# Three small edits to an attention and MLP block: a PSUM buffer, the place of twelve matmuls, and a quarter of an add on GpSimd

## The chip, the cores and the metric

The kernel runs on one core of a Trainium2 chip. The metric is the device time of one execution in microseconds (us), the median over several executions. A single core has no dies to compare, so a run here counts as fast unless it lies over 1.5% above the fastest of its kernel, which none did; the state of e7, which ran once, is unknown.

## The reference, cut to what matters

```
mod = (silu(c) @ w_mod).reshape(...)          # sa, ca, ga, sb, cb, gb, each 512 long
h = layernorm(x) * (1 + ca) + sa              # x is 2048 x 512
q = h @ wq                                    # 32 heads of 128
o = softmax(q k^T / sqrt(128)) v              # 8 groups of keys and values, 2048 keys
x = x + ga * (o @ wo)
h = layernorm(x) * (1 + cb) + sb
z = gelu(h @ w_in)                            # 1792 wide: halves z1, z2
g = w_sp @ layernorm(z2) + b_sp
x = x + gb * ((z1 * g) @ w_out)
```

## The kernel before

Attention is cut into 128 units, one for each group of keys (8) and tile of 128 query rows (16). A unit has 8 slots. In a slot PE (TensorE) writes two score blocks for this unit, ACT (ScalarE) takes their exponential, PE multiplies earlier exponentials of the unit before with the values, and then come "fill" matmuls that belong to something else:

```python
for it in range(NU + 6):
    ...
    for i in range(NSLOT):                       # NSLOT = 8
        for fn in later.pop((it, i), []):
            fn()
        if it < NU:
            qk(it, i)                            # 2 score matmuls, then exp on ACT
        if 1 <= it <= NU:
            pv(it - 1, i)                        # 8 value matmuls
        for fn in fill.pop((it, i), []):
            fn()                                 # projections, warm-up and the like
```

PSUM has three tags, each with two buffers: `misc` and `o_ps` (one bank each) and `s_ps` (two banks). Who takes a buffer waits until the reader of that buffer's last content is done.

```python
psum = fast.enter_context(tc.tile_pool(name="psum", bufs=2, space=bass.MemoryType.PSUM))
def bank(name):
    return psum.tile([P, 512], FP32, name=name)
```

Three places matter. First, in unit 0 normalised rows are turned (transposed) on PE, in two halves, and DVE (VectorE) scales each half on its way to SBUF:

```python
def ln1_turn(j0, n, xns):
    ...
    for half in range(2):
        t_ps = bank("misc")[:].bitcast(BF16).rearrange("p (k q) -> p k q", k=2)
        for k in range(2):
            ...
            nc.tensor.transpose(...)             # line 827
        for k in range(2):
            ln1_mod(dst, src, dt)                # line 809, DVE
```

Second, the queries of units 2 and 3 are projected by sixteen matmuls, `rest_q`, on line 940. The eighth and the sixteenth are each followed by a DVE cast into `qT` (line 951). Four run in unit 0, the others are fill of unit 1:

```python
rest_q = qproj(0, [0, 1], 2 * P, 2 * P) + qproj(0, [2, 3], 2 * P, 2 * P)
fill[0, 7] = rest_q[0:4]
for i in range(6):
    fill[1, i] = rest_q[4 + 2 * i : 6 + 2 * i]
```

Third, the end of each output tile:

```python
nc.vector.tensor_tensor(out=tmp[:], in0=src, in1=gb_rows[:], op=ALU.mult)       # src in PSUM
nc.vector.tensor_tensor(out=yout[:], in0=tmp[:], in1=x_sb[:, j, :], op=ALU.add)
nc.scalar.dma_start(out=out_dram[:, j, :], in_=yout[:])
```

## Time and profile before

| | before |
|---|---|
| median of 3 runs | 1321.84 us (1321.56 to 1321.89) |
| span of the profiled run | 1320.0 us |
| PE busy | 1311.8 us, 99% |
| score matmuls begin | 10.65 us |
| last store issued | 1316.01 us |

The page's groups of instructions (line, engine, operation, output and inputs, count, then busy us, mean ns of one, and idle time before with what ended it) show where the time is:

```profile
L980 ACT ACTIVATE pT<-s_ps 128x1024 bf16<-128x1024 f32 x1024 | 1043.8, 1024 | 82.5 <-PE s_ps L973 7.4
...
L973 PE MATMUL s_ps<-qT,kT 128*128 128x512 bf16 x2048 | 609.1, 379 | 0.6 <-ACT pT L980 0.5
```

ACT's exponentials cover 1044 of 1320 us, so ACT is the next busiest after PE. PE's score matmuls waited 0.6 us in all. The number to compare is the pitch in steady work: a slot without fill takes PE 0.885 us, an exponential 0.917 us, and two fill matmuls of 256 columns add 0.215 us to PE. PE is the slower of the two in most units, ACT only in slots without fill.

### The profile page before, as it was taken

The page shows a single profiled execution, that of the slowest core. Times are in us where ns is not written, and L with a number is a line of the kernel's source. Part 1 is how long each engine was busy: PE and PEld are TensorE (multiplying, and loading weights), DVE is VectorE, ACT ScalarE, POOL GpSimd, SP SyncE. Part 2 cuts the span into 40 slices and gives each one's busy share as a digit, 9 for nine tenths or more (in the row PEclk, how much of TensorE's full clock was granted, in tenths as well). Part 3 has the DMA queues.
Part 4 walks back from the last instruction along what each step waited for, and adds up shares of the span by engine and source line. Part 5 has one row for each costly group of instructions (what it writes and reads, how often), then busy time and mean ns, then how long its engine had stood idle before and what let it go on. Part 6 is the DMA issues. An engine that isn't in the chain of part 4 may idle for free.

```text
span 1320.0 us, 27930 instructions
## 1 busy us (share of the span) xinstructions
PE 1311.8 (99%) x12359; PEld 857.8 (65%) x12359; DVE 471.7 (36%) x1162; ACT 1077.1 (82%) x1061; POOL 51.8 (4%) x96
## 2 busy tenths in 40 slices
PE   9999999999999999999999999999999999999998
PEld 5666666666666666666666666666666666644445
DVE  5622222222222222222222222222222566794444
ACT  7899999999999999999999999999999999650000
POOL 1201000000000000000000000000000000020000
PEclk9999999999999999999999999999999999999999
DMA  7542121112101111211111211121111112143300
GB/s 180 141 104 47 20 45 37 37 17 50 37 17 37 30 37 37 33 33 38 33 37 13 53 38 33 18 53 22 32 14 21 25 31 33 33 112 84 69 21 26
DMA packets 148944, 58.64 MB, mean 44 GB/s; under 512 B 138480, under 2 KB 144880, under 8 KB 148816
## 3 DMA queue, kind: packets, MB, share of 16 engines
q1 hardware_dynamic: 141792, 37.65, 15.6%
q0 software_dynamic: 4432, 16.91, 4.5%
q8 instruction: 98, 1.61, 0.5%
q10 hardware_dynamic: 2592, 2.23, 0.5%
q14 instruction: 30, 0.25, 0.1%
HBM read 21.89 MB, written 2.10 MB: 18 GB/s over the span
## 4 chain that ended last, share of the span: by engine, by line
PE 99%; DMA 0%; DVE 0%; ACT 0%; SPq 0%; issue 0%; DVEq 0%
PE o_ps L995 35%; PE s_ps L973 34%; PE misc L1027 8%; PE misc L940 8%; PE misc L1336 7%; PE s_ps L1182 2%; PE s_ps L1221 2%; PE o_ps L1357 1%; PE s_ps L1357 1%; DMA wmod_a<-in_w_mod_dram 0%; PE misc L850 0%; ACT pT L980 0%; PE misc L1344 0%; PE o_ps L781 0%; PE misc L827 0%; DVE qT L951 0%
## 5 line engine op out<-in xcount | busy, mean ns | idle before, releaser
L980 ACT ACTIVATE pT<-s_ps 128x1024 bf16<-128x1024 f32 x1024 | 1043.8, 1024 | 82.5 <-PE s_ps L973 7.4
L995 PEld LDWEIGHTS <-pT 128*128 128x128 bf16 x8192 | 548.2, 98 | 241.5
L995 PE MATMUL o_ps<-v,pT 128*128 128x129 bf16 x8192 | 631.7, 220 | 0.0
L973 PE MATMUL s_ps<-qT,kT 128*128 128x512 bf16 x2048 | 609.1, 379 | 0.6 <-ACT pT L980 0.5
L1006 DVE RECIPROCAL rall<-o_ps 128x2 f32<-128x2 f32 x256 | 43.7, 171 | 742.9 <-PE o_ps L995 739.5
L973 PEld LDWEIGHTS <-kT 128*128 128x128 bf16 x2048 | 199.0, 98 | 119.6 <-issue 1.0
L1027 PE MATMUL misc<-wo_g,oT 128*128 128x512 bf16 x512 | 194.2, 379 | 0.0
L940 PE MATMUL misc<-hT,wq_g 128*128 128x512 bf16 (+2 forms) x528 | 190.3, 371 | 0.0
L1007 DVE TENSOR_TENSOR onorm<-o_ps,rall 128x256 bf16<-128x256 f32 x256 | 108.7, 425 | 8.8
L1336 PE MATMUL misc<-wsp,z 128*128 128x512 bf16 (+2 forms) x560 | 100.7, 337 | 0.0
L951 DVE CAST qT<-misc 128x512 bf16<-128x512 f32 x127 | 86.4, 681 | 3.1 <-PE misc L940 3.1
L1336 PEld LDWEIGHTS <-z 128*128 128x128 bf16 x560 | 50.5, 98 | 48.5
L1040 DVE TENSOR_TENSOR xacc<-misc,xacc 128x512 f32<-128x512 f32 x112 | 76.2, 680 | 0.0
L940 PEld LDWEIGHTS <-wq_g 128*128 128x128 bf16 x528 | 50.4, 98 | 0.8
L1027 PEld LDWEIGHTS <-oT 128*128 128x128 bf16 x512 | 50.0, 98 | 0.9
L1351 DVE TENSOR_TENSOR gb<-misc,bsp_bc 128x512 bf16<-128x512 f32 (+1 forms) x28 | 18.4, 658 | 58.5 <-PE misc L1336 58.5
L1182 PE MATMUL s_ps<-win_sb,hT 128*128 128x448 bf16 x128 | 27.0, 353 | 0.0
L1192 ACT ACTIVATE z<-s_ps 128x896 bf16<-128x896 f32 x16 | 14.7, 917 | 14.9 <-PE s_ps L1182 14.9
L1221 PE MATMUL s_ps<-hT,win_sb 128*128 128x512 bf16 x112 | 24.5, 379 | 0.0
L1229 ACT ACTIVATE z1T<-s_ps 128x1024 bf16<-128x1024 f32 x14 | 14.3, 1024 | 10.1 <-PE s_ps L1221 9.1
L692 DVE BATCH_NORM_STATS2 bnst<-x_sb 128x6 f32<-128x512 bf16 x32 | 21.9, 683 | 1.3 <-DMA x_sb<-in_A_x_dram 0.8
L1357 PE MATMUL o_ps<-wout_sb,yT 128*128 128x512 bf16 x84 | 20.1, 379 | 0.0
(86 smaller groups left out, 268.9 us busy)
## 6 DMA issues: line engine op xcount, KB each, us to landing
wq_g<-in_A_wq_dram POOLq DMA_DIRECT2D x7, 512.0 KB, 3.9
v<-in_A_v_cache_dram POOLq DMA_DIRECT2D x7, 512.0 KB, 5.8
wo_g<-in_A_wo_dram POOLq DMA_DIRECT2D x7, 512.0 KB, 4.7
oT<-onorm SPq DMA_TRANSPOSE x128, 2.4
wsp<-in_w_mod_dram POOLq DMA_DIRECT2D x1, 2048.0 KB, 11.8
out_dram<-yout ACTq DMA_DIRECT2D x16, 128.0 KB, 1.7
win_sb<-in_B_w_in_dram POOLq DMA_DIRECT2D x1, 1792.0 KB, 7.7
x_sb<-in_A_x_dram SPq DMA_DIRECT2D x3, 512.0 KB, 5.6
```

Source lines behind the costliest of these rows:

```text
L940: nc.tensor.matmul(ps[0][:, o0 : o0 + n], lhsT=wqs[g][:, dt, hh * DH : (hh + 1) * DH], rhs=hTs[ch][:, dt, c0 : c0 + n], start=(dt == 0), s ...
L951: nc.vector.tensor_copy(out=dst, in_=src)
L973: nc.tensor.matmul(s_ps[:, h * 512 : (h + 1) * 512].rearrange("p (r q) -> p r q", r=REP), lhsT=groups[g]["kT"][:, kt * P : (kt + 1) * P], ...
L980: nc.scalar.activation(out=pTs[u][:, 2 * i : 2 * i + 2, :], in_=s_ps[:].rearrange("p (k q) -> p k q", k=2), func=ACT.Exp, scale=inv_sqrt_dh,)
L995: nc.tensor.matmul(o_ps[:, hh % 2, 0 : DH + 1], lhsT=pTs[u][:, kt, hh * P : (hh + 1) * P], rhs=groups[g]["v1"][:, kt, 0 : DH + 1], start=( ...
L1007: nc.vector.tensor_tensor(out=onorms[u][:, hh - 1 : hh + 1, :], in0=o_ps[:, :, 0:DH], in1=rall[:, c0 : c0 + 2].unsqueeze(2).to_broadcast([ ...
L1027: nc.tensor.matmul(X_ps[:], lhsT=oTs[u][:, hh, :], rhs=groups[g]["wo"][:, hh, :], start=(hh == 0), stop=(hh == REP - 1),)
L1040: nc.vector.tensor_tensor(out=xaccs[j][:], in0=X_ps[:], in1=xaccs[j][:], op=ALU.add)
L1182: nc.tensor.matmul(ps[0][:, hf * 512 : hf * 512 + FC], lhsT=h2Ts[j // CT][:, dt, (j % CT) * P : (j % CT + 1) * P], rhs=win_sb[:, dt, FH + ...
L1221: nc.tensor.matmul(ps[0][:, k * 512 : (k + 1) * 512], lhsT=win_sb[:, dt, f * P : (f + 1) * P], rhs=h2Ts[2 * ch2 + k][:, dt, :], start=(dt ...
L1336: nc.tensor.matmul(g_ps[:, :n], lhsT=z2[:, st, f * P : (f + 1) * P], rhs=wsp[t][:, st, c0 : c0 + n], start=(st == 0), stop=(st == NT - 1 a ...
L1357: nc.tensor.matmul(dst, lhsT=yT[:, f, jj * P : (jj + 1) * P], rhs=wout_sb[:, f, :], start=(f == 0), stop=(f == NFT - 1),)
```

## The change

The intent, as the edits show it: let the second half of a turn take a buffer nobody reads; spread the projections evenly over unit 1, so that no slot of it is without fill; and shorten the last DVE add by giving a quarter of it to Pool (GpSimd).

```diff
-            t_ps = bank("misc")[:].bitcast(BF16).rearrange("p (k q) -> p k q", k=2)
+            t_ps = bank(("misc", "o_ps")[half])[:].bitcast(BF16).rearrange("p (k q) -> p k q", k=2)
...
-    for i in range(6):
-        fill[1, i] = rest_q[4 + 2 * i : 6 + 2 * i]
+    for i in range(NSLOT):
+        fill[1, i] = rest_q[4 + 3 * i // 2 : 4 + 3 * (i + 1) // 2]
...
-    def finish_tile(t, jj, src):
+    def finish_tile(t, jj, src, pool_cols=0):
...
-        nc.vector.tensor_tensor(out=yout[:], in0=tmp[:], in1=x_sb[:, j, :], op=ALU.add)
+        for engine, c0, c1 in (
+            (nc.gpsimd, D - pool_cols, D),
+            (nc.vector, 0, D - pool_cols),
+        ):
+            if c1 > c0:
+                engine.tensor_tensor(
+                    out=yout[:, c0:c1], in0=tmp[:, c0:c1], in1=x_sb[:, j, c0:c1], op=ALU.add
+                )
...
-    finish_tile(last, CT - 1, o2_last[CT - 1])
+    finish_tile(last, CT - 1, o2_last[CT - 1], pool_cols=P)
```

## The prediction

> **What bounds the kernel now.** I read the page first, for the share of each engine and the chain that ended last; then the table of waits of PE, for what is left to win; then the timeline at the three places the change touches.
>
> ```profile
> PE 1311.8 (99%) x12359; PEld 857.8 (65%) x12359; DVE 471.7 (36%) x1162; ACT 1077.1 (82%) x1061; POOL 51.8 (4%) x96
> ...
> PE 99%; DMA 0%; DVE 0%; ACT 0%; SPq 0%; issue 0%; DVEq 0%
> ```
>
> TensorE (PE) is busy for 1311.8 of 1320.0 us and is 99% of the chain. A busy PE is not a PE at its peak, but here it says that whatever does not open or close a gap on PE moves nothing. The change takes no matmul away. So the gaps are the whole stake, and the table of PE's waits lists them:
>
> ```profile
> PE o_ps L781 <- DVE onorm L763: 1.2, 1, 1.2
> PE misc L827 <- DVE qT L951: 0.6, 1, 0.6
> PE s_ps L973 <- ACT pT L980: 0.5, 2, 0.2
> PE misc L850 <- DMA wmod_a<-in_w_mod_dram: 0.2, 1, 0.2
> ```
>
> Columns: waiter, what ended the wait, total us, times, longest. The second line is the only one that the first part of the change can remove. No edit can win over 2% (26 us) where PE waits for 2.5 us in all; the last 4 us of the span are an output transfer.
>
> The wait in its place, from the timeline between 16 and 19 us (start, us, engine, line, operation; in brackets the idle time before it and what ended it):
>
> ```profile
> 16.05 0.39 PE L827 MATMUL misc<-ident,xn 128*128 128x128 bf16 x4
> 16.25 0.69 DVE L951 CAST qT<-misc 128x512 bf16<-128x512 f32 x1 [0.51 <-PE misc L940]
> 16.86 1.36 DVE L809 TENSOR_SCALAR hT<-misc,modc 128x256 bf16<-128x256 bf16 x4
> 17.00 0.39 PE L827 MATMUL misc<-ident,xn 128*128 128x128 bf16 x4 [0.56 <-DVE qT L951]
> ...
> 18.93 0.38 PE L973 MATMUL s_ps<-qT,kT 128*128 128x512 bf16 x1 [0.24 <-ACT pT L980]
> ```
>
> The second half of the transposes stands until the qT cast has ended at 16.94, because `misc` has two buffers and the cast still reads the one it needs. Also to be seen: when the cast's reader is PE, PE goes 0.06 us after the cast ends, and a cast starts 0.03 us after the last matmul's result (16.22).
>
> Unit 2 of the attention begins here, in the timeline between 26.8 and 28.3 us:
>
> ```profile
> 26.86 0.62 PE L995 MATMUL o_ps<-v,pT 128*128 128x129 bf16 x8
> ...
> 27.31 0.60 PE L973 MATMUL s_ps<-qT,kT 128*128 128x512 bf16 x2
> 27.51 0.17 DVE L1006 RECIPROCAL rall<-o_ps 128x2 f32<-128x2 f32 x1 [1.08 <-PE o_ps L995]
> ...
> 27.72 0.42 DVE L1007 TENSOR_TENSOR onorm<-o_ps,rall 128x256 bf16<-128x256 f32 x1
> ```
>
> PE passes from unit 1 to unit 2 without a gap (8 matmuls issued in 0.45 us, their results 0.17 later), while DVE normalises what they wrote.
>
> The end of the kernel, in the timeline after 1313 us:
>
> ```profile
> 1314.56 0.69 DVE L1369 TENSOR_TENSOR tmp<-s_ps,gb_rows 128x512 f32<-128x512 f32 x1 [0.48 <-PE s_ps L1357]
> 1315.29 0.69 DVE L1370 TENSOR_TENSOR yout<-tmp,x_sb 128x512 bf16<-128x512 f32 x1
> ```
>
> Here DVE alone sets the end: multiply, add, then the last store.
>
> **What the Trainium skill says.** (1) "PSUM — Partial Sum Buffer", section Engine vs sequencer instructions: matmuls start and complete in program order. So a matmul that waits for DVE holds back the independent ones behind it. The trace agrees: at 16.44 to 17.00 the score matmuls (L973) behind the waiting transposes waited too, though exp had freed their buffer at 15.87 (it ran from 11.28 at 0.917 us per tile). (2) "SBUF — State Buffer", section Who interferes with whom: a VectorE instruction with two SBUF inputs contends with a GpSimd instruction that reads SBUF, and the second one blocks until the first has finished. The last add has two SBUF inputs (tmp, x_sb), and Pool's quarter reads the same two. No instruction pair of this exact kind overlaps in the trace. Near it, the timeline of POOL shows the same operation alone, and then beside DVE's normalisation:
>
> ```profile
> 1172.15 1.04 POOL L677 TENSOR_TENSOR rstd_lnz<-ve_lnz,mhalf 128x4 f32<-128x4 f32 x1
> ...
> 1178.57 1.58 POOL L677 TENSOR_TENSOR rstd_lnz<-ve_lnz,mhalf 128x4 f32<-128x4 f32 x1 [1.33 <-DVE z L681]
> ```
>
> It took 1.58 instead of 1.04 us, which fits blocking but does not prove it. (3) "GPSIMD Engine Reference", section 3.1, Elementwise: a two-input elementwise operation takes about 2.6 cycles of 1.2 GHz per element. For 128 columns that is 0.28 us, an estimate; with dispatch I take 0.35. The trace has no such operation on Pool.
>
> **Part by part.** First, the transposes. With the second half in `o_ps`, the built program has it wait only for an earlier PE write. Its four issue at 16.27, and the scores for slot 6 follow at about 16.5 instead of 17.22; exp follows at 17.1 instead of 17.85. The next hold is the four L940 projections, which need all four scaled pieces from DVE; these are behind the cast in DVE's order either way and end at 18.22. So the fourth projection issues at 18.27 and the scores of unit 1 at 18.38, where before they waited for exp until 18.93. Won: 0.55 us, less than the 0.75 that exp gains.
>
> Second, the spread. Twelve projection matmuls remain twelve (0.107 us each), so unit 1 takes 8.38 us of PE either way (18.93 to 27.31 before). What moves is the last pair: from slot 5 to slot 7, after which the first score matmul of unit 2 reads the very heads that they produce. The instruction order of the changed kernel shows it: that score matmul's weight load now waits for DVE, and DVE's order there is reciprocal, normalise, cast. Call the last result of L995 zero. Reciprocal at 0.03; normalise at 0.24 (27.51 to 27.72 before); the operation behind such a normalise starts 0.34 after it (46.07 to 46.41 in the timeline of DVE), so the cast at 0.58; it takes 0.69, to 1.27; PE goes at 1.33. Without the wait PE would go at -0.17 plus two projections, 0.21, so 0.04. Added: 1.29 us. Exp cannot hide it: it takes 0.917 per tile, and unit 1's slots average 1.05 on PE, so exp is idle before it as well. A credit: in unit 2 before, slots 1 to 4 lasted 3.63 us (28.20 to 31.83) where PE needs 4 x 0.885 = 3.54, since exp limits them; after a pause PE needs no such wait. Won: 0.09. Net cost: 1.20.
>
> Third, the tail. DVE's add on 384 columns takes 0.69 x 0.81 = 0.56 (a 128x384 L1351 of this trace takes 0.56, a 128x512 one 0.69): 0.13 won if Pool runs beside it (Pool from about 1315.34 to 1315.69, DVE to 1315.85). If one blocks the other, both end near 1316.25: 0.27 lost. I give blocking 6 in 10: expected +0.11.
>
> Sum: 1321.84 - 0.55 + 1.20 + 0.11 = 1322.6; I round towards the side of doubt, to 1322.5.
>
> **The rivals.** (a) The cast's wait is hidden, because exp is behind by that point or DVE is early; then only the gains are left, 1321.84 - 0.55 - 0.09 and -0.13 to +0.27, so 1321.1 to 1321.5. For it: someone spread these projections on purpose, and exp limits the unfilled slots. Against: PE's two units of idle-free pitch, and the wait that is in the program. (b) The gain of the transposes is lost in the next hold too (exp or DVE's scaling): then 1322.9 to 1323.3. For it: DVE's order is not changed, and its 18.22 stays. Against: before, the hold was exp's end at 18.88, which moves with the scores. (c) The two adds run side by side: 1322.4 with my other terms, 1322.8 with blocking.
>
> **Range and chances.** My middle runs 1322.4 to 1322.8; (b) adds half a microsecond above, (a) takes about one away. Three runs before lie within 0.33 us. I put 1321.6 to 1323.1, giving (a) a little over one in ten. All of it is under 0.15%: within 2% is all but certain.
>
> **What would show it.** Right: PE's wait of L827 for the cast is gone and L973 of unit 1 starts near 18.4; a new line, PE s_ps L973 waiting for DVE qT L951, about 1.3 us, once, near 27 us; unit 2's slot 5 about 0.65 us later than 31.83; at the end Pool's add starting or ending after DVE's 0.56 us add. Wrong: no such wait of L973, or one under 0.5 us; a start of unit 1 no earlier than 18.8; or a later stage whose gaps change, which nothing here predicts.

## The result, and the profile after

The changed kernel took 1322.51 us (median of 6 runs, 1322.17 to 1322.98), the kernel before 1321.88 us in its 6 runs. The ratio of the fast runs is 1.0005 with a 95% interval of 0.9992 to 1.0018. Such a ratio is the mean time of one kernel's fast runs over that of the other's of the same rounds, so it is not quite the ratio of the medians. By the 2% rule the verdict is "same", and even the sign lies inside the interval; what the signs rest on is the traces.

PE's waits in the changed kernel (waiter, releaser, us in total, times, longest):

```profile
PE o_ps L781 <- DVE onorm L763: 1.2, 1, 1.2
PE s_ps L973 <- DVE qT L951: 1.1, 1, 1.1
PE misc L850 <- DMA wmod_a<-in_w_mod_dram: 0.4, 1, 0.4
PE s_ps L973 <- ACT pT L980: 0.2, 1, 0.2
```

The wait of L827 for the cast is gone, and a longer one for the same kind of cast has come, on the score matmuls. The place where the first of these two waits was, in the timeline of the changed kernel between 15.6 and 18.1 us:

```profile
15.67 0.39 PE L827 MATMUL misc<-ident,xn 128*128 128x128 bf16 x4
15.87 0.69 DVE L951 CAST qT<-misc 128x512 bf16<-128x512 f32 x1 [0.51 <-PE misc L940]
15.89 0.39 PE L827 MATMUL o_ps<-ident,xn 128*128 128x128 bf16 x4
...
16.98 1.18 PE L940 MATMUL misc<-hT,wq_g 128*128 128x256 bf16 x4
...
18.00 0.59 PE L973 MATMUL s_ps<-qT,kT 128*128 128x512 bf16 x2
```

The second four transposes go out 0.22 us after the first four, beside the cast. All times are 0.39 us earlier than in the trace of before, because the first score matmul came at 10.26 instead of 10.65 us; the traces of the experiments show that this start differs by more than that, even between two of one build. Counted from that matmul, unit 1 begins at 7.74 us; before it was 8.28.

The pass to unit 2, in the timeline between 26 and 28.5 us:

```profile
26.17 0.38 PE L940 MATMUL misc<-hT,wq_g 128*128 128x256 bf16 x2
26.37 0.17 DVE L1006 RECIPROCAL rall<-o_ps 128x2 f32<-128x2 f32 x1 [1.32 <-PE o_ps L995]
26.57 0.42 DVE L1007 TENSOR_TENSOR onorm<-o_ps,rall 128x256 bf16<-128x256 f32 x1
26.91 0.68 DVE L951 CAST qT<-misc 128x512 bf16<-128x512 f32 x1
27.65 0.61 PE L973 MATMUL s_ps<-qT,kT 128*128 128x512 bf16 x2 [1.10 <-DVE qT L951]
...
28.36 1.94 ACT L980 ACTIVATE pT<-s_ps 128x1024 bf16<-128x1024 f32 x2 [1.42 <-PE s_ps L973]
```

The projections that end at slot 7 are the last work of PE before it needs their cast. DVE first does the reciprocal and the normalise. ACT idles 1.42 us over the same stretch, so it had no backlog to hide behind.

The end:

```profile
1314.91 0.69 DVE L1369 TENSOR_TENSOR tmp<-s_ps,gb_rows 128x512 f32<-128x512 f32 x1 [0.48 <-PE s_ps L1357]
1315.64 0.56 DVE L1375 TENSOR_TENSOR yout<-tmp,x_sb 128x384 bf16<-128x384 f32 x1
1315.68 0.80 POOL L1375 TENSOR_TENSOR yout<-tmp,x_sb 128x128 bf16<-128x128 f32 x1 [127.06 <-DVE tmp L1369]
```

DVE's share is done at 1316.20, Pool's at 1316.48. An undivided add would have ended at 1315.64 + 0.69 = 1316.33.

One warning about views. The page of before gave a chain that was 99% PE. In the changed kernel the last instruction that the view starts from is Pool's, and the view does not get back past its program order:

```profile
issue 0%; POOL 0%; POOLq 0%
POOL yout L1375 0%; POOLq L1428 0%
```

Such a page does not mean that Pool bounds the kernel. The other views still read as before.

### The profile page after: what moved, and what is told of

Its sections match the earlier page's. It is cut to its first block, busy times and chain, and to the rows that moved or that the text cites. A ratio compares the mean times of both kernels' runs of the same rounds, so it can differ in the third digit from the quotient of the medians.

```text
span 1320.5 us, 27933 instructions
## 1 busy us (share of the span) xinstructions
PE 1311.6 (99%) x12359; PEld 858.2 (65%) x12359; DVE 471.3 (36%) x1162; ACT 1077.2 (82%) x1061; POOL 52.2 (4%) x97
```

## The experiments

Ten runs on three chips. Because the start moves from execution to execution, the table counts from the first score matmul of the kernel: "unit 1" and "unit 2" are the first score matmul of that unit, and "store" is the issue of the last store. The last column is the difference of the medians. Kernels are compared only within the same rounds. All results were correct.

| run | unit 1 | unit 2 | store | store against before | median against before |
|---|---|---|---|---|---|
| before | 8.28 | 16.66 | 1305.36 | | |
| e0_after | 7.73 | 17.38 | 1306.23 | +0.87 | +0.74 |
| e1_turn | 7.73 | 16.12 | 1304.82 | -0.54 | -0.52 |
| e2_spread | 8.28 | 17.93 | 1306.63 | +1.27 | +1.50 |
| e3_pool | 8.27 | 16.66 | 1305.51 | +0.15 | +0.18 |
| e4_turn_spread7 | 7.73 | 16.18 | 1304.88 | -0.48 | -0.85 |
| e5_pool_quarter_first | 8.28 | 16.66 | 1305.33 | -0.03 | +0.10 |
| e6_spread_early | 8.27 | 17.15 | 1305.86 | +0.50 | +0.09 |
| e7_pool_half | 8.28 | 16.67 | 1305.62 | +0.26 | +0.70 (one run) |
| e8_turn_quarter_first | 7.73 | 16.12 | 1304.80 | -0.56 | -0.36 |
| e9_turn_again | 7.73 | 16.12 | 1304.81 | -0.55 | -0.66 |

The medians scatter around the traces by up to 0.4 us; no single ratio is clear of 1 (e7, with one execution, has none). What the traces say repeats: the same build (e1 and e9) gives the same distances within 0.01 us.

**The changed kernel again.** No edit.

> The changed kernel again, on the chip that runs its parts, so that the parts can be added up on one chip. Theory (turn -0.55, cast's wait +1.29, tail +0.15 as its first trace shows): 0.5 to 0.9 us slower than the kernel before, 1322.4 to 1322.7. In the trace, from the first score matmul of the kernel: unit 1 starts 7.73 us after it (8.28 before), unit 2 17.38 after it (16.66 before). Rival (the slowdown is chance between chips or builds): no difference over 0.2 us.

It took 1322.29 us against 1321.55, ratio 1.0006 (0.9993 to 1.002). Unit 1 begins at 7.73 and unit 2 at 17.38, as in the first trace of the change. Counted from the first score matmul, the two traces of this kernel agree within 0.02 us. So the rival, that the slowdown is chance between chips or builds, falls as far as distances in a trace go; the ratio alone would not exclude it.

**The turn alone.**

```diff
-            t_ps = bank("misc")[:].bitcast(BF16).rearrange("p (k q) -> p k q", k=2)
+            t_ps = bank(("misc", "o_ps")[half])[:].bitcast(BF16).rearrange("p (k q) -> p k q", k=2)
```

> Only the transposes' second half in the other pool. Theory: unit 1's first score matmul 7.73 us after the first score matmul of the kernel instead of 8.28, unit 2's 16.11 after it instead of 16.66, and all of the 0.55 us kept to the end: about 1321.3. Rival (the lead is given back where exp limits the slots that have no projections, or at the next wait for a scaled tile): under 0.2 us, about 1321.7.

1321.03 us, ratio 0.9996 (0.9983 to 1.001). Unit 1 gains 0.55 us and the store still has 0.54 of it. The rival that something later takes it back falls.

**The spread alone.**

```diff
+    for i in range(NSLOT):
+        fill[1, i] = rest_q[4 + 3 * i // 2 : 4 + 3 * (i + 1) // 2]
```

> Only the projections spread over eight slots of unit 1. Theory: one wait of a score matmul for the qT cast, 1.1 to 1.3 us, so unit 2 starts 17.95 us after the first score matmul instead of 16.66; the total 1.2 to 1.3 us longer, about 1323.1. Rival (the wait costs only in company with the earlier unit 1 of the first part, or exp absorbs it): within 0.3 us of the kernel before.

1323.05 us, ratio 1.0011 (0.9997 to 1.0024). Its waits have both casts, the old one on the transposes and the new one on the scores:

```profile
PE s_ps L973 <- DVE qT L951: 1.1, 1, 1.1
...
PE misc L827 <- DVE qT L951: 0.6, 1, 0.6
```

Unit 2 begins 1.27 us later and the store is 1.27 us later. The wait does not depend on the earlier unit 1 of the first part, and nothing absorbs it.

**Pool's quarter alone.** The `finish_tile` edit of the change.

> Only Pool's quarter of the last add. Theory (Pool's add is held until DVE's add ends): Pool's record about 0.8 us, store issued 1.60 us after the last multiply starts instead of 1.45, total 0.15 us longer, about 1322.0. Rival (run to run spread hides a gain; the two run side by side): store issued after 1.32 us, total 0.13 shorter.

1321.73 us, ratio 1.0002 (0.9988 to 1.0016). Pool's record is 0.80 us and the store goes 1.60 us after the last multiply starts; before it was 1.45. The time does not resolve 0.15 us; the trace does. In the traces the three parts sum to -0.54 + 1.27 + 0.15 = 0.88, and the whole change has 0.87.

**The spread over seven slots, with the turn.** It keeps the even spreading and moves the last pair one slot away from its reader.

```diff
+    for i in range(7):
+        fill[1, i] = rest_q[4 + 12 * i // 7 : 4 + 12 * (i + 1) // 7]
```

> The transposes' part, and the projections spread over seven slots instead of eight, so that the last pair ends one slot (0.885 us of matmuls) before unit 2 reads it. Theory (only the wait for the cast costs, not the spreading): no wait of a score matmul for the cast over 0.15 us; unit 2 starts 16.11 to 16.2 us after the first score matmul; total about 1321.3, as with the transposes alone. Rival (spreading itself costs, say because exp gets uneven gaps): about 1322.

1321.05 us, ratio 0.9994 (0.998 to 1.0008). No wait for the cast is in its list. Unit 2 starts at 16.18, 0.06 later than with the turn alone. Its timeline:

```profile
26.15 0.69 DVE L951 CAST qT<-misc 128x512 bf16<-128x512 f32 x1 [0.66 <-PE misc L940]
...
26.90 0.61 PE L973 MATMUL s_ps<-qT,kT 128*128 128x512 bf16 x2
```

The cast runs beside the last slot's matmuls and ends at 26.84; the scores follow at 26.90, as far behind it as PE follows a cast in the prediction's reading (0.06 us). So the cast still held them, and the 0.06 us lost is a rest of the wait, too short for the list. It is the place of the last pair that costs, not the spreading; but the spreading gained nothing either.

**Pool's quarter multiplied first.** Here Pool's add runs beside a DVE instruction with one SBUF operand.

```diff
-        nc.vector.tensor_tensor(out=tmp[:], in0=src, in1=gb_rows[:], op=ALU.mult)
+        cuts = (D - pool_cols, D), (0, D - pool_cols)
+        for c0, c1 in cuts:
+            if c1 > c0:
+                nc.vector.tensor_tensor(
+                    out=tmp[:, c0:c1], in0=src[:, c0:c1], in1=gb_rows[:, c0:c1], op=ALU.mult
+                )
```

> Pool's quarter as in the change, but DVE multiplies that quarter first, so that Pool's add runs beside a DVE multiply that reads one operand from PSUM and one from SBUF. Theory (in the change Pool's add is held by DVE's add, which has two SBUF operands): Pool's record falls from 0.80 to about 0.3 us. Rival (Pool's add of 128 columns simply takes 0.80 us): the record stays at 0.80. The total: DVE takes 0.29 + 0.56 + 0.56 with gaps, store issued about 1.52 us after the first multiply starts instead of 1.45, so 0.07 us slower than before, 1321.9 to 1322.0.

```profile
1314.94 0.75 DVE L1372 TENSOR_TENSOR tmp<-s_ps,gb_rows 128x128 f32<-128x128 f32 x2 [0.48 <-PE s_ps L1357]
1315.31 0.43 POOL L1380 TENSOR_TENSOR yout<-tmp,x_sb 128x128 bf16<-128x128 f32 x1 [126.64 <-DVE tmp L1372]
1315.73 0.56 DVE L1380 TENSOR_TENSOR yout<-tmp,x_sb 128x384 bf16<-128x384 f32 x1
```

The same Pool instruction takes 0.43 us, not 0.80. So 0.37 us of the 0.80 came from what ran beside it. In the change that was an add which has two SBUF operands and reads the very tiles that Pool reads; these runs do not tell the two apart. That it is shorter is the theory's mark, though 0.43 is more than the 0.3 expected. The expectation for the total was wrong in its sign: I had added 0.29 and 0.56 with a gap, but two independent DVE multiplies overlap and take 0.75 together. The store goes 1.42 us after the first multiply starts, 0.03 sooner than before. It comes 0.08 us after the end of DVE's add, where in the other kernels it follows the last add by 0.03. The time, 1322.00 against 1321.90, cannot show that.

**The last pair in front of the value matmuls**, in slot 7 of unit 1, with the spread of the change and without the turn.

```diff
             if it < NU:
                 qk(it, i)
+            if (it, i) == (1, NSLOT - 1):
+                for fn in fill.pop((it, i)):
+                    fn()
             if 1 <= it <= NU:
                 pv(it - 1, i)
```

> Projections over eight slots, without the transposes' part, but in the last slot of unit 1 the pair is issued in front of the eight value matmuls. Theory (the 1.29 us is result latency, normalise and cast, in DVE's order): the cast now comes in front of the normalise and 0.45 us of matmuls lie beside it, so PE waits about 0.5 us and the total is about 1322.3. Rival (the wait is a fixed cost of a change of unit, or the cast itself is slow to be seen by PE): still 1.1 us or more, 1323.

```profile
26.91 0.62 PE L995 MATMUL o_ps<-v,pT 128*128 128x129 bf16 x8
27.10 0.69 DVE L951 CAST qT<-misc 128x512 bf16<-128x512 f32 x1 [1.64 <-PE misc L940]
...
27.85 0.61 PE L973 MATMUL s_ps<-qT,kT 128*128 128x512 bf16 x2 [0.33 <-DVE qT L951]
```

The cast now comes first on DVE, and PE does value matmuls beside it. Unit 2 starts 0.49 us later than before instead of 1.27. The wait is the sum of what stands in DVE's order less what PE can do meanwhile; it is not a fixed price. The time, 1321.99 us against 1321.90, is lower than the 0.5 expected and within the scatter.

**Pool's half.** `pool_cols=2 * P`.

> Pool adds half of the last tile (256 columns) instead of a quarter. Theory (held until DVE's 256-column add ends, 0.42 us, then 2.6 cycles of 1.2 GHz per column, 0.55 us, an estimate with the figure of GPSIMD Engine Reference, section 3.1): Pool's record about 0.9 to 1.0 us, store issued about 1.75 us after the multiply starts. Rival (Pool not held, 0.80 us per 128 columns): record near 1.6 us, store after about 2.4 us.

```profile
1315.63 0.42 DVE L1375 TENSOR_TENSOR yout<-tmp,x_sb 128x256 bf16<-128x256 f32 x1
1315.67 0.90 POOL L1375 TENSOR_TENSOR yout<-tmp,x_sb 128x256 bf16<-128x256 f32 x1 [127.02 <-DVE tmp L1369]
```

Twice the columns lengthen Pool's record from 0.80 to 0.90 us only. A Pool that is merely slow does not fit this. Counted from the end of DVE's add, Pool needs 1316.57 - 1316.05 = 0.52 us for 256 columns and 0.28 us (1316.48 - 1316.20) for 128 in the change: it is held, then takes about 0.24 us per 128 columns. The store went 1.71 us after the multiply, 1.75 was expected.

**The two gains together, and the turn again.** e8 has the edits of e1 and e5, e9 is the kernel of e1.

> The two edits that gained in the traces together: the transposes' second half in the other pool (0.54 us in the trace of that part alone) and the last quarter multiplied first, so that Pool's add runs beside a multiply (add ended 1.35 us after the first multiply started, 1.42 before: 0.07). Theory (the two lie far apart and add up): last multiply starts 1303.37 us after the first score matmul, add ends 1.35 us later, total 0.6 us shorter than before. Rival (the gain of the tail was chance of one trace): add ends 1.42 us or more after the multiply starts.

> The transposes' part alone, once more, as the measure for the run before it and for the start: the same build had its first score matmul at 10.91 us. If the start belongs to the build it comes at 10.9 again; if it is chance of the run, anywhere between 10.1 and 11.1. Total 0.5 us shorter than before; distances from the first score matmul as before (7.73, 16.12).

e8 took 1321.29 us (1320.83 to 1321.73), ratio 0.9997 (0.9984 to 1.0011); e9 1320.99 us (1320.67 to 1321.22), ratio 0.9995 (0.9981 to 1.0009), against 1321.65 us. In its trace e8's add ends 1.35 us after the first multiply starts, as expected, but its store goes only after 1.43, 0.02 sooner than without Pool: of the 0.07 us that the add gained, the store keeps 0.02, and as a time this is not to be seen. The first score matmul of e9 came at 10.39 us on chip 1, that of the same build in e1 at 10.91 on chip 2, where four builds lay between 10.15 and 10.91. So neither the build nor the chip alone sets the start; no build has two traces that are known to be of one chip. Over all twelve traces it lies between 10.15 and 11.03 us. That is as wide as the change's whole effect. The turn alone is the version to keep: its traces beat both kernels, both of its medians are below those of before, and what e4 and e8 add to it gains at most 0.02 us.

## Why the prediction was right or wrong

The time was 1322.51 us where 1322.5 was predicted, inside the range. That is luck: the start alone moves 0.9 us, and the terms of the sum gave 0.76 us (1322.6 before it was rounded) where the traces have 0.88. The steps say more.

- **The turn.** Right in cause and size: 0.55 us was predicted, unit 1 begins 0.54 earlier in the change and 0.55 in the turn alone, and the store keeps it. The next hold was the four scaled pieces, as said: the last projection and the scores at 18.00 are 18.39 on before's count, where 18.38 stood in the working. Rival (b), that the gain is lost in that hold, falls with e1.
- **The spread.** The mechanism was right, shown by e2 (the cost alone), e4 (the place moved by one slot, 0.06 left) and e6 (the order changed, 0.49 left). The size was 1.27 for 1.29 predicted. The table of waits gives 1.1 because it counts idle time from the modelled end of the projections, 0.17 us after their issue; the spacing of starts is the cost. Rival (a), that exp hides the wait, falls: ACT was idle 1.42 us there.
- **The credit of 0.09 us in unit 2** is the term that was wrong. From the first score matmul of unit 2 to that of its slot 5 took 4.53 us in the change (27.65 to 32.18) and 4.52 before. The sign, slot 5 about 0.65 us later than 31.83, came 0.74 later on before's count (32.18 + 0.39 = 32.57). The prediction took it that exp, after a pause, would no longer limit the slots. But exp had not come into unit 2 behind in the kernel before either: there its first exponential starts 0.69 us after the first score matmul, in the change 0.70. So the pause gave exp no lead, and it limits three slots at 0.917 again. Part of those 0.7 us is an instruction that waits for a semaphore on ACT, in front of the first exponential of the units from unit 2 on, in both kernels. A view of the trace of before lists it:

```profile
L980 ACTq EVENT_SEMAPHORE  x126: 17/17/17, 27.9 to 1129.0; - x126
```

  Where ACT waited for the scores, exp started 0.476 us (median of 125) after the second score matmul of its slot behind such an instruction, and 0.416 us (median of 741) without one. The first unit has none: 0.63 us there (10.65 to 11.28). An estimate from these starts: had exp begun 0.06 us earlier, the change would have won about 0.06 of the 0.09 us. No run took the instruction out.
- **The tail.** Blocking was put at 6 in 10, and it is what the runs support: 0.80 us beside DVE's two-SBUF-operand add, 0.43 beside the multiply, 0.90 for twice the columns. The size was off: 0.27 predicted for the blocked case, 0.15 measured at the store. I had counted Pool's whole 0.35 us, and a gap of 0.05, after DVE's end; only 0.28 comes after it. Rival (c), both side by side, falls.
- **The sum.** In the traces the whole is 0.87 to 0.89 us, with the blocked branch my terms gave 0.92. They come close because two errors cancel: the credit of 0.09 that did not come, and a tail that was put 0.12 too high. The median difference was 0.63 in the first comparison and 0.74 in e0; the start, 0.39 us earlier in the profiled run of the change than in that of before, can account for a difference of this size, but the start of the other executions was not recorded.

## What to carry to other kernels

When fill work is moved to even out slots, look at who reads its result: the last piece needs other work between it and the reader, long enough for result latency, what stands ahead on DVE, and the cast. Here one slot of 0.885 us fell short by 0.06. A wait on a double buffer at one place can be freed by a buffer of another tag that is idle there: the wait of 0.56 us gave back 0.55. Before a part of a DVE operation goes to Pool, look at what DVE does beside it: next to the add with two SBUF operands Pool's quarter cost 0.15 us, next to the multiply it gained 0.03 at most. Where effects are under a thousandth, distances within a trace decide, not times.

## What the Trainium skill lacked or had wrong

- "SBUF — State Buffer", Who interferes with whom: right, as far as these runs go, that a GpSimd read is held by a VectorE instruction with two SBUF inputs. It does not say how a profile shows it: Pool's record starts on time and is stretched, 0.80 us for 0.43, and no wait for DVE's add is named.
- "GPSIMD Engine Reference", section 3.1, gives about 2.6 cycles per element for two inputs of fp32; with one fp32 and one bf16 input, 128 more columns took 0.24 us more after the release, which is 2.25 cycles of 1.2 GHz per column. Its example has 2048 elements; at 128 columns the whole instruction took 0.43 us, where the rate alone gives 0.28.
- None of the pages cited here gives the time that an instruction waiting for a semaphore costs ACT: the first exponential of a unit started 0.476 us after its second score matmul behind one, against 0.416 us without (medians of 125 and 741 in the trace of before).
- "PSUM — Partial Sum Buffer", on matmuls in program order: nothing to correct; the scores behind the waiting transposes moved from 6.57 to 5.86 us after the first score matmul (17.22 - 10.65 and 16.12 - 10.26).
